# Attention loads as transfers over 128 partitions, with heads paired by parity, in a banded attention and feed-forward kernel

## The chip, the cores and the metric

The kernel runs on one core of one Trainium2 chip. The metric is the device time of one execution in microseconds (us), the median over several runs; lower is better. The profile shows one execution of its own. Engines are named as the profile names them: PE (matrix products), DVE, ACT and POOL (vector, scalar and general work), SP (here it only issues DMA transfers). The 16 DMA engines of the core move data between the chip's main memory (HBM) and the on-chip memory of 128 partitions.

## The reference: what is computed

Two stages. The first is attention with a band: 8 batches of 576 positions, 8 heads of width 64, and each position sees itself and the 63 positions before it. The second is a feed-forward layer over the 4608 resulting tokens, with a leaky slope per hidden unit.

```python
scores = scale * np.matmul(q, k.transpose(0, 1, 3, 2))
mask = (rel >= 0) & (rel < 64)
scores = np.where(mask, scores, -1000000000.0)
attn = np.exp(scores - np.max(scores, axis=-1, keepdims=True))
attn = attn / (np.sum(attn, axis=-1, keepdims=True) + 1e-09)
x = (attn @ v)                      # to 4608 x 512
h = x @ w_in                        # 4608 x 2048
g = np.maximum(h, 0.0) + alpha * np.minimum(h, 0.0)
out = g @ w_out                     # 4608 x 512
```

All of it is in float32. The feed-forward weights are split in the kernel into a high and a low part, and each product is the sum of three.

## The kernel before, in words

**Tiles.** The 4608 tokens are 36 tiles of 128, in nine groups of four (NBLK). Attention of a tile `t` (function `attend`) reads its queries `q`, the keys `k` of its two blocks of 64 positions and the block before them, and the values `v` of the same blocks. PE makes the scores `s` (32 small products), DVE masks them and takes the maximum, ACT exponentiates, DVE and POOL normalise, PE (for tiles 0 to 7) or DVE (later tiles) transposes the weights into `pt`, PE multiplies with the values into `av`, ACT and DVE split the result into `xh` and `xl`.

**Cells.** The feed-forward of a group is 16 cells (function `cell`), one for each 128 hidden units `f`. A cell makes `h` on PE (from `xh`, `xl`, `win_h`, `win_l`), `g`, `gh` and `gl` on ACT, DVE and POOL, and adds twelve products to `o` on PE (`wout_h`, `wout_l`). For the first four `f` group 0 runs two cells of two tiles each. PE is in order: cells of a group, with the attention steps of later tiles between them.

**Weights.** 32 weight tiles of 512 KB (function `weights`; tile c is `w_in` for even c, `w_out` for odd c, and belongs to f = c / 2) are fetched into `raw`, of which there are three buffers, and converted by ACT, DVE and POOL: `two`, `low`, `val`, then `win_h` and `win_l`, or `wout_h` and `wout_l`. A cell needs both tiles of its f. This happens once, during group 0.

**Loads.** In the host's arrays a head pair `e` holds two heads; `qT` and `kT` have 64 rows (the head's width) for each pair, `vN` has 64 rows (the positions of a block) for each pair and each block. In the chip's memory the pairs 0 and 1 of q and k lie in partitions 0 to 63 and the pairs 2 and 3 in 64 to 127, and the values of a tile's first block lie in the lower half, those of the block after it in the upper. Each half is a DMA of its own: four for q and k of a tile and two for its values. The first four tiles are loaded two at a time (`span`). All are issued by SP, except the keys of the first two tiles, which ACT issues. A value buffer is reused by the next tile, so in the steady stage values can load only after the previous tile's `av`.

**What sets the order.** Every piece of work is a `Step` with engines, times, predecessors and buffers. `Plan.order` places the steps greedily by their modelled times, and the resulting order is the order of the program on each engine, SP among them. A load's `moved` is its modelled transfer time; the model has one common transfer lane, and at most eight transfers in flight (FLIGHT). The program waits through eight DMA semaphores, taken in turn, so an issue can wait for the transfer eight places earlier to land. A buffer named `z...` is used by the first loads and then inherited by the last weights (`LATE`).

Of the kernel before, what the change touches and what calls it, by code (L numbers as in the profile page):

```python
# [44 lines left out]
class Plan:  # L45
# [107 lines left out]
def banded_attention_then_prelu_ffn(  # L153
# [85 lines left out]
    def weights(c):  # L239
# [80 lines left out]
    def attend(t, by_pe, want, loads_behind=(), behind=(), last=None):  # L320

        d = st[t]
        early = t < 2
        wb, pb = Buffer("w", 2 if by_pe else 1), Buffer("pt", 1)

        span = 2 if t < NBLK else 1
        own = t % span
        t0 = t - own
        if own == 0:
            if span == 2:  # L330
                j = t // 2
                qb = kb = Buffer(f"z{2 + j}", 2, f"late z{2 + j}")
                vb = Buffer(f"z{j}", 2, f"late z{j}")
            else:
                qb, kb, vb = Buffer("q", 1), Buffer("k", 1), Buffer("v", 1)
            NW = 2 * span + 1
            loads, lv = [], []

            def rooms():
                if span == 2:  # L340
                    both = room(qb, [P, 2, span * 2 * P + NW * 2 * W], F32, f"qk_{t}")
                    d["q"], d["k"] = both[:, :, :span * 2 * P], both[:, :, span * 2 * P:]
                else:
                    d["q"] = room(qb, [P, 2, span * 2 * P], F32, f"q_{t}")
                    d["k"] = room(kb, [P, 2, NW * 2 * W], F32, f"k_{t}")

            for x in range(2):
                r = slice(x * D, (x + 1) * D)

                def load_q(e, x=x, r=r):  # L350
                    if x == 0:
                        rooms()
                    nc.sync.dma_start(d["q"][r], qT[2 * x:2 * x + 2, :, t:t + span].rearrange("e d t h q -> d e (t h q)"))

                def load_k(e, x=x, r=r):
# [3 lines left out]
                loads.append(step({SP: (0.62, 0.62)}, load_q, (), [*loads_behind, *loads[-1:]],  # L359
                                  take=([qb] if span == 2 else [qb, kb]) if x == 0 else [], moved=0.88 if span == 2 else 0.6))  # L360
                loads.append(step({ACT if t == 0 else SP: (0.62, 0.62)}, load_k, (), [*loads_behind, *loads[-1:]],
                                  moved=1.02 if span == 2 else 0.73))
            for u in range(2):
                def load_v(_, u=u):
                    if u == 0:
                        d["v"] = room(vb, [P, NP, 2 * span, P], F32, f"v_{t}")
                    nc.sync.dma_start(d["v"][u * W:(u + 1) * W].rearrange("w c b d -> w c (b d)"),
                                      vN[:, :, 2 * t + u:2 * t + u + 2 * span].rearrange("c w b d -> w c (b d)"))
                lv.append(step({SP: (0.62, 0.62)}, load_v, (), [*loads_behind, *lv[:1]], take=[vb] if u == 0 else [],
                               moved=1.76 if span == 2 else 1.18))  # L370
            d["from"] = loads, lv, qb, kb, vb
        loads, lv, qb, kb, vb = st[t0]["from"]

        banks = [Buffer("o" if early else "bank", NP) for _ in range(2)]

        def score(_):
            d["w"] = room(wb, [P, NH, KW], F32, f"w_{t}")
            for x in ("nm", "sm", "rc"):
                d[x] = sb.tile([P, NH], F32, tag=f"{x}{t % 2}", name=f"{x}_{t}")
            d["s"] = [bank(banks[x], [P, 2, 2, KW], F32, f"s_{t}_{x}") for x in range(2)]  # L380
            q = st[t0]["q"].rearrange("p y (t h q) -> p y t h q", h=2, q=P)
            k = st[t0]["k"].rearrange("p y (b h w) -> p y b h w", h=2, w=W)
            for u in range(2):
                for y in range(2):
                    for h in range(2):
                        for x in range(2):
                            r = slice(x * D, (x + 1) * D)
                            nc.tensor.matmul(d["s"][x][h * W:(h + 1) * W, u, y], q[r, y, own, h, u * W:(u + 1) * W],  # L388
                                             k[r, y, 2 * own + u:2 * own + u + 2, h, :], start=True, stop=True)

        cold = 1.0 + 0.9 * (t < 2)
        sc = step({PE: (1.05 * cold, 1.15 * cold)}, score, loads, behind, take=[*banks, wb],
                  give=[qb] if qb is kb else [qb, kb])
        sc.tiled = True
        if last:
            follow(sc, last)
# [1 line left out]
        for u in range(2):  # L398
            some = []
            for e in range(NP):  # L400
                g = u * NP + e

                def mask(_, u=u, e=e, g=g):
                    m = masks[:, 1 if (t * P + u * W) % seq == 0 else 0, :]
                    nc.vector.tensor_tensor_reduce(  # L405
                        out=d["w"][:, g, :], in0=d["s"][e // 2][:, u, e % 2], in1=m, op0=ALU.add, op1=ALU.min,
                        scale=-SCALE, scalar=3.0e38, accum_out=d["nm"][:, g:g + 1])
# [6 lines left out]
                m = step({DVE: (0.21, 0.37)}, mask, [sc], give=[banks[e // 2]])  # L414
                some.append(step({ACT: (0.385, 0.58)}, soft, [m]))
            sums.append(some)

# [56 lines left out]
        def value(_):  # L474
            d["av"] = av = bank(ab, [P, NP, P], F32, f"av_{t}")
            for e in range(NP):
                for u in range(2):
                    for h in range(2):
                        r = slice(h * D, (h + 1) * D)
                        nc.tensor.matmul(av[r, e, u * W:(u + 1) * W], st[t0]["v"][:, e, 2 * own + u, r],  # L480
                                         d["pt"][:, u * NP + e, h * W:(h + 1) * W], start=True, stop=True)

        def x_high(_):
# [1 line left out]

        def x_low(_):
            nc.vector.tensor_tensor(out=xl[:, :, xs], in0=d["av"], in1=xh[:, :, xs].bitcast(F32), op=ALU.subtract)  # L487

        va = step({PE: (1.08 * cold, 1.2 * cold)}, value, lv + ready, take=[ab], give=[vb, pb])
        va.tiled = True  # L490
# [207 lines left out]
```

## Time and profile before

| what | value |
|---|---|
| median of 3 runs | 920.09 us (919.77 to 922.85) |
| the profiled execution, its own time | 917.98 us |
| its span, first to last instruction | 916.2 us |
| PE busy | 892.2 us, 97% of the span |
| DVE, ACT, POOL busy | 445.6, 382.7, 313.6 us |
| packets moved | 54121, 69.42 MB |
| queue of SP's transfers | 53728 packets, 67.78 MB, 26.5% of 16 engines' span |

An engine's busy time is the sum of its instructions; it is an average over stages with different limits. PE's row in the strip of 40 slices reads `4799999999999999999999999999999999999998`: it is less than 90% busy in the first two slices and the last. The strip of the DMA engines reads `9787645021312123212311131213121221001001`, busy in the first 160 us and light after. "Share" of the DMA engines is the mean busy share of the 16. A wait is written as "who waited <- for whom: us in all, times, longest". In rows of the trace the first two numbers are the start and the length in us.

### The profile page before, as it was taken

The numbers are of one execution on the slowest core, as the hardware profiler recorded it, in microseconds if no ns is written. First come the engines' busy times: TensorE is split into PE (matmuls) and PEld (weight loads), VectorE is DVE, ScalarE is ACT, GpSimd is POOL, SyncE is SP. The second block draws the span as 40 slices with busy tenths as digits, with TensorE's granted clock in tenths as the row PEclk, the third lists the DMA queues.
The fourth block names the chain that finished last, engine by engine and source line by source line (L and its number), as shares of the span: only waits on it lengthen the run. The fifth ranks groups of instructions, "written<-read, shape, count | busy, mean of one in ns | idle before, by whom it ended". The sixth has DMA issues, their size and how long they took to land.

```text
span 916.2 us, 15392 instructions
## 1 busy us (share of the span) xinstructions
PE 892.2 (97%) x5873; PEld 727.5 (79%) x5873; DVE 445.6 (49%) x1315; ACT 382.7 (42%) x1020; POOL 313.6 (34%) x243
## 2 busy tenths in 40 slices
PE   4799999999999999999999999999999999999998
PEld 3687778888888888888888888888888888888886
DVE  3988984644544444444444444445444544422111
ACT  3887874333433343333433333334333433322222
POOL 3677783223322332233222333233323332322221
PEclk9999999999999999999999999999999999999999
DMA  9787645021312123212311131213121221001001
GB/s 224 180 219 205 198 144 151 24 53 52 99 53 52 52 56 96 52 52 52 98 34 42 38 92 52 53 53 99 53 52 53 70 80 53 1 1 47 1 1 46
DMA packets 54121, 69.42 MB, mean 76 GB/s; under 512 B 4368, under 2 KB 45344, under 8 KB 54048
## 3 DMA queue, kind: packets, MB, share of 16 engines
q1 hardware_dynamic: 53728, 67.78, 26.5%
q8 instruction: 46, 0.75, 0.3%
q10 hardware_dynamic: 320, 0.66, 0.3%
q14 instruction: 27, 0.22, 0.1%
HBM read 58.99 MB, written 9.44 MB: 75 GB/s over the span
## 4 chain that ended last, share of the span: by engine, by line
PE 90%; DMA 3%; ACT 3%; DVE 2%; issue 1%; POOL 1%; POOLq 0%; SPq 0%; ACTq 0%; DVEq 0%
PE h L519 42%; PE o L552 41%; PE av L480 4%; PE s L388 3%; DMA raw<-w_in 1%; DMA qk<-kT 1%; DMA raw<-w_out 1%; PE t L444 1%; ACT w L411 1%; ACT low L273 0%; ACT win_h L296 0%; DVE val L277 0%; POOL val L281 0%; DVE two L260 0%; DVE win_l L300 0%
## 5 line engine op out<-in xcount | busy, mean ns | idle before, releaser
L537 POOL TENSOR_TENSOR gl<-g,gh 128x512 fp32r<-128x512 f32 (+1 forms) x135 | 173.3, 1284 | 421.7 <-ACT gh L533 421.6
L528 DVE SCALAR_TENSOR_TENSOR g<-h,s_sb,g 128x512 f32<-128x512 f32 (+1 forms) x148 | 108.9, 736 | 292.2 <-ACT g L525 291.9
L525 ACT ACTIVATE g<-h,sa_sb 128x512 f32<-128x512 f32 (+1 forms) x148 | 100.3, 678 | 334.5 <-PE h L519 332.4
L552 PE MATMUL o<-wout_h,gh 128*128 128x512 f32 x576 | 226.6, 393 | 0.0
L552 PE MATMUL o<-wout_l,gh 128*128 128x512 f32 x576 | 226.3, 393 | 0.0
L519 PE MATMUL h<-xh,win_h 128*128 128x512 f32 (+1 forms) x592 | 160.2, 392 | 3.7 <-DVE xl L487 1.8
L465 DVE STREAM_TRANSPOSE pt<-w 32x256 f32<-32x256 f32 x336 | 146.6, 436 | 31.0 <-POOL w L427 26.1
L552 PE MATMUL o<-wout_h,gl 128*128 128x512 f32 x576 | 160.6, 392 | 0.4 <-POOL gl L537 0.4
L519 PE MATMUL h<-xl,win_h 128*128 128x512 f32 (+1 forms) x592 | 155.3, 384 | 0.0
L519 PE MATMUL h<-xh,win_l 128*128 128x512 f32 (+1 forms) x592 | 154.8, 383 | 0.0
L411 ACT ACTIVATE w<-w,nm 128x128 f32<-128x128 f32 x288 | 112.1, 392 | 62.7 <-DVE nm L405 62.7
L533 ACT CAST gh<-g 128x512 fp32r<-128x512 f32 (+1 forms) x148 | 90.0, 608 | 107.4 <-DVE g L528 107.3
L519 PEld LDWEIGHTS h<-xh,win_h 128*128 128x128 f32 x592 | 106.6, 188 | 27.9 <-DVE xl L487 1.9
L552 PEld LDWEIGHTS o<-wout_h,gl 128*128 128x128 f32 x576 | 108.2, 188 | 25.0 <-POOL gl L537 0.8
L519 PEld LDWEIGHTS h<-xl,win_h 128*128 128x128 f32 x592 | 109.5, 188 | 22.9
L519 PEld LDWEIGHTS h<-xh,win_l 128*128 128x128 f32 x592 | 109.5, 188 | 22.1
L552 PEld LDWEIGHTS o<-wout_h,gh 128*128 128x128 f32 x576 | 108.2, 188 | 23.6 <-ACT g L525 0.3
L552 PEld LDWEIGHTS o<-wout_l,gh 128*128 128x128 f32 x576 | 108.2, 188 | 23.2
L427 POOL TENSOR_TENSOR w<-w,rc 128x1024 f32<-128x1024 f32 (+1 forms) x44 | 70.6, 1607 | 150.5 <-DVE rc L423 149.2
L405 DVE CUSTOM_DVE_ANT_0 w<-s,masks 128x128 f32<-128x128 f32 x288 | 63.9, 286 | 68.0 <-PE s L388 68.0
L411 ACT ACTIVATION_READ_ACCUMULATOR w<-w,nm 128x1 f32 x288 | 54.5, 189 | 0.0
L281 POOL TENSOR_TENSOR val<-val,low 128x512 int32<-128x512 int32 x32 | 42.6, 1339 | 12.5 <-DVE val L277 8.4
(48 smaller groups left out, 460.5 us busy)
## 6 DMA issues: line engine op xcount, KB each, us to landing
v<-vN SPq DMA_DIRECT2D x64, 256.0 KB, 4.2
k<-kT SPq DMA_DIRECT2D x64, 192.0 KB, 3.5
out<-os SPq DMA_DIRECT2D x36, 256.0 KB, 2.2
raw<-w_in SPq DMA_DIRECT2D x16, 512.0 KB, 4.7
raw<-w_out SPq DMA_DIRECT2D x16, 512.0 KB, 4.4
q<-qT SPq DMA_DIRECT2D x64, 128.0 KB, 3.1
v<-vN SPq DMA_DIRECT2D x4, 512.0 KB, 11.6
qk<-qT SPq DMA_DIRECT2D x4, 256.0 KB, 9.1
```

Source lines behind the costliest of these rows:

```text
L281: nc.gpsimd.tensor_tensor(out=d["val"], in0=d["val"], in1=d["tail"], op=ALU.add)
L405: nc.vector.tensor_tensor_reduce(out=d["w"][:, g, :], in0=d["s"][e // 2][:, u, e % 2], in1=m, op0=ALU.add, op1=ALU.min, scale=-SCALE, scal ...
L411: nc.scalar.activation(w, w, AF.Exp, scale=-1.0, bias=d["nm"][:, g:g + 1], accum_out=d["sm"][:, g:g + 1])
L427: nc.gpsimd.tensor_tensor(out=w, in0=w, in1=d["rc"][:, g].unsqueeze(2).broadcast_to(list(w.shape)), op=ALU.mult)
L465: nc.vector.transpose(d["pt"][ks, :, r], d["w"][r, :, ks])
L480: nc.tensor.matmul(av[r, e, u * W:(u + 1) * W], st[t0]["v"][:, e, 2 * own + u, r], d["pt"][:, u * NP + e, h * W:(h + 1) * W], start=True, ...
L519: nc.tensor.matmul(ph[:, :nt], weight(wt, f)[:, c * P:(c + 1) * P], xt[:, c, xs], start=(k == 0), stop=(k == 3 * NP - 1))
L525: nc.scalar.activation(d["g"], d["h"][:, :nt], AF.Copy, scale=sa_sb[:, f:f + 1])
L528: nc.vector.scalar_tensor_tensor(out=d["g"], in0=d["h"][:, :nt], scalar=s_sb[:, f:f + 1], in1=d["g"], op0=ALU.mult, op1=ALU.max)
L533: nc.scalar.copy(d["gh"], d["g"])
L537: (nc.gpsimd if e == POOL else nc.vector).tensor_tensor(out=d["gl"], in0=d["g"], in1=d["gh"].bitcast(F32), op=ALU.subtract)
L552: nc.tensor.matmul(po[t][0], gt[:, i * P:(i + 1) * P], weight(wt, f), start=(f == 0 and k == 0), stop=(f == NF - 1 and k == 2))
```

## The change

Loads of queries, keys and values are written anew.

- **Queries and keys.** Pairs go to the halves by parity: pair `2y + x` lies in half `x` at place `y`. The rows of both halves then follow one another at one stride in HBM, and one DMA over 128 partitions brings the q of a tile and one its k.
- **Values.** One DMA for each head pair. Its destination is 128 partitions; its source is written by hand as `[[P, 2], [row stride, 64], [1, 256]]`: two halves whose starts differ by one block, 64 rows, and 256 numbers in a row. The second half reads one block on, so the two overlap.
- **One queue.** All of these are issued by SP. Tiles are loaded one at a time, the first four too. Rooms for the first tiles are given by a table (`ROOMS`), and the late parts of the weights are eight pieces of two hidden blocks instead of four pieces of four or five.
- **Scores.** Pair `e` is found in bank `e % 2` at place `e // 2`, where it was the other way round.
- **The planner's figures.** Initial times of the engines, `moved` of the weight tiles and of the loads.

```diff
-        free = {e: 0.0 for e in (PE, DVE, ACT, POOL, SP)}
+        free = {PE: 0.0, DVE: 0.0, ACT: 0.8, POOL: 3.6, SP: 0.8}
...
-LATE = (("wout_h", 12, "z0"), ("wout_l", 12, "z1"), ("win_h", 11, "z2"), ("win_l", 11, "z3"))
+LATE = (("wout_h", 12, "z0"), ("wout_h", 14, "z1"), ("wout_l", 12, "z2"), ("wout_l", 14, "z3"),
+        ("win_h", 12, "z4"), ("win_h", 14, "z5"), ("win_l", 12, "z6"), ("win_l", 14, "z7"))
+ROOMS = {0: ("q", "k", "z0"), 1: ("q", "k", "z1"), 2: ("z4", "z5", "z2"), 3: ("z6", "z7", "z3")}
...
-        s0 = step({SP: (0.4, 0.4)}, fetch, take=[raw], moved=1.3 if odd else 2.4)
+        s0 = step({SP: (0.4, 0.4)}, fetch, take=[raw], moved=1.27 if odd else 1.47)
...
-                    nc.sync.dma_start(d["q"][r], qT[2 * x:2 * x + 2, :, t:t + span].rearrange("e d t h q -> d e (t h q)"))
...
-                    (nc.scalar if e == ACT else nc.sync).dma_start(
-                        d["k"][r], kT[2 * x:2 * x + 2, :, 2 * t:2 * t + NW].rearrange("e d b h w -> d e (b h w)"))
...
-                    nc.sync.dma_start(d["v"][u * W:(u + 1) * W].rearrange("w c b d -> w c (b d)"),
-                                      vN[:, :, 2 * t + u:2 * t + u + 2 * span].rearrange("c w b d -> w c (b d)"))
...
+            (nc.scalar if e == ACT else nc.sync).dma_start(
+                d["q"], qT[:, :, t].rearrange("(y x) d h q -> (x d) y (h q)", x=2))
...
+            nc.sync.dma_start(d["k"], kT[:, :, 2 * t:2 * t + 3].rearrange("(y x) d b h w -> (x d) y (b h w)", x=2))
+
+        loads = [step({SP: (0.62, 0.62)}, load_q, (), loads_behind, take=[qb], moved=0.75),
+                 step({SP: (0.62, 0.62)}, load_k, (), loads_behind, take=[kb], moved=1.05)]
+        lv = []
+        for e in range(NP):
+            def load_v(_, e=e):
+                if e == 0:
+                    d["v"] = room(vb, [P, NP, 2, P], F32, f"v_{t}")
+                src = vN[e, :, 2 * t:2 * t + 2].rearrange("w b d -> w (b d)")
+                src = bass.AP(src.tensor, src.offset, [[P, 2], *map(list, src.ap)])
+                nc.sync.dma_start(d["v"][:, e].rearrange("p b d -> p (b d)"), src)
+            lv.append(step({SP: (0.62, 0.62)}, load_v, (), [*loads_behind, *lv[:1]], take=[vb] if e == 0 else [],
+                           moved=0.38))
...
-                        out=d["w"][:, g, :], in0=d["s"][e // 2][:, u, e % 2], in1=m, op0=ALU.add, op1=ALU.min,
+                        out=d["w"][:, g, :], in0=d["s"][e % 2][:, u, e // 2], in1=m, op0=ALU.add, op1=ALU.min,
```

The order that the planner makes changes with it. Of three places the rows are shown; the first number of a name is the tile, or for `raw` the weight tile c.

SP before, from the start of the program up to the weight tile raw_3 (the keys of tiles 0 and 1 are on ACT's queue):

```order
L353 DMA qk_0_96<-qT 64x2x512 x2
L367 DMA v_0_101<-vN 64x4x512 x2
L249 DMA raw_0_104<-w_in 128x4x256
L353 DMA qk_2_108<-qT 64x2x512
L356 DMA qk_2_108<-kT 64x2x640
L353 DMA qk_2_108<-qT 64x2x512
L356 DMA qk_2_108<-kT 64x2x640
L249 DMA raw_2_117<-w_in 128x4x256
L249 DMA raw_1_141<-w_out 128x1024
L367 DMA v_2_173<-vN 64x4x512 x2
L249 DMA raw_4_248<-w_in 128x4x256
L249 DMA raw_3_366<-w_out 128x1024
```

SP with the change, up to the same weight tile; four rows stand ahead of these, k and q of tile 0 and of tile 1:

```order
L348 DMA v_0_104<-vN 128x1x256 x4
L251 DMA raw_0_137<-w_in 128x4x256
L337 DMA k_2_139<-kT 128x2x384
L332 DMA q_2_141<-qT 128x2x256
L348 DMA v_1_165<-vN 128x1x256 x4
L251 DMA raw_1_186<-w_out 128x1024
L337 DMA k_3_192<-kT 128x2x384
L251 DMA raw_2_199<-w_in 128x4x256
L332 DMA q_3_212<-qT 128x2x256
L348 DMA v_2_219<-vN 128x1x256 x4
L348 DMA v_3_265<-vN 128x1x256 x2
L251 DMA raw_3_302<-w_out 128x1024
```

Ahead of raw_3 stood four value DMAs of 512 KB and now stand fourteen of 128 KB; raw_4 has moved behind it.

DVE before, around the split `xl` of tile 1 (`w_3` are the masks of tile 3, `pt` copies of transposed weights, `two` the first conversion of a weight tile):

```order
L405 ISA w_3_306,nm_3_307<-s_3_1_311,masks_64 128x128
L405 ISA nm_3_307 128x1
L451 COPY pt_0_92<-t_2_0_372 128x512
L487 TENSOR_TENSOR xl_91<-av_1_334,xh_90 128x4x128
L451 COPY pt_0_92<-t_2_1_385 128x512
L422 TENSOR_SCALAR rc_3_309<-sm_3_308 128x4
L423 RECIPROCAL rc_3_309<-rc_3_309 128x4
L260 TENSOR_SCALAR two_4_414<-raw_4_248 128x512
L260 TENSOR_SCALAR two_3_435<-raw_3_366 128x512
```

DVE with the change, first where the conversion of raw_3 begins (eight masks of tile 3 follow it, with `val` of raw_2 between), then around the same `xl`:

```order
L399 TENSOR_SCALAR rc_2_244<-sm_2_243 128x4
L400 RECIPROCAL rc_2_244<-rc_2_244 128x4
L262 TENSOR_SCALAR two_3_366<-raw_3_302 128x512
L382 ISA w_3_336,nm_3_337<-s_3_0_340,masks_64 128x128
L382 ISA nm_3_337 128x1
```

```order
L399 TENSOR_SCALAR rc_3_339<-sm_3_338 128x4
L400 RECIPROCAL rc_3_339<-rc_3_339 128x4
L267 TENSOR_SCALAR two_3_366<-two_3_366,flip_sb_84 128x512
L464 TENSOR_TENSOR xl_91<-av_1_368,xh_90 128x4x128
L262 TENSOR_SCALAR two_4_424<-raw_4_362 128x512
```

The first conversion of raw_3 stood five rows behind `xl` of tile 1 and now stands ahead of it and ahead of the masks of tile 3.

PE, whose order up to the first cell is the same in both; with the change it reads there (`h_0_0` is the first cell's):

```order
L457 MATMUL av_1_368<-pt_0_92,v_1_165 64x64 x16
L421 MATMUL t_2_0_404<-ident_79,w_2_241 128x128 x4
L421 MATMUL t_2_1_417<-ident_79,w_2_241 128x128 x4
L497 MATMUL h_0_0_426<-xh_90,win_h_86 128x256 x4
L497 MATMUL h_0_0_426<-xl_91,win_h_86 128x256 x4
L497 MATMUL h_0_0_426<-xh_90,win_l_87 128x256 x4
```

Nothing has moved here: the first cell stands behind `av` of tile 1 and the transposes of tile 2, and reads the `xl` of tiles 0 and 1.

Further on, SP issues the values of tile 4 between raw_10 and raw_9, those of tile 5 around raw_16, those of tile 6 around raw_23, and those of tile 7 behind raw_31, the last weight tile.

More of the change, by code (lines that the diff above doesn't have):

```diff
@@ L324, in attend @@
         wb, pb = Buffer("w", 2 if by_pe else 1), Buffer("pt", 1)
[L326 to L352, printed above, removed]
-                    nc.sync.dma_start(d["q"][r], qT[2 * x:2 * x + 2, :, t:t + span].rearrange("e d t h q -> d e (t h q)"))
-                def load_k(e, x=x, r=r):
-                    (nc.scalar if e == ACT else nc.sync).dma_start(
-                        d["k"][r], kT[2 * x:2 * x + 2, :, 2 * t:2 * t + NW].rearrange("e d b h w -> d e (b h w)"))
[L359 to L367, printed above, removed]
-                                      vN[:, :, 2 * t + u:2 * t + u + 2 * span].rearrange("c w b d -> w c (b d)"))
-                lv.append(step({SP: (0.62, 0.62)}, load_v, (), [*loads_behind, *lv[:1]], take=[vb] if u == 0 else [],
-                               moved=1.76 if span == 2 else 1.18))
-            d["from"] = loads, lv, qb, kb, vb
@@ L372, in attend, with load_q, load_k @@
-        loads, lv, qb, kb, vb = st[t0]["from"]
+        qb, kb, vb = (Buffer(z, 1, "late " + z if z[0] == "z" else None) for z in ROOMS.get(t, ("q", "k", "v")))
+        def load_q(e):
+            d["q"] = room(qb, [P, 2, 2 * P], F32, f"q_{t}")
+            (nc.scalar if e == ACT else nc.sync).dma_start(
+                d["q"], qT[:, :, t].rearrange("(y x) d h q -> (x d) y (h q)", x=2))
+        def load_k(_):
+            d["k"] = room(kb, [P, 2, 6 * W], F32, f"k_{t}")
+            nc.sync.dma_start(d["k"], kT[:, :, 2 * t:2 * t + 3].rearrange("(y x) d b h w -> (x d) y (b h w)", x=2))
@@ L380, in score @@
             d["s"] = [bank(banks[x], [P, 2, 2, KW], F32, f"s_{t}_{x}") for x in range(2)]
-            q = st[t0]["q"].rearrange("p y (t h q) -> p y t h q", h=2, q=P)
-            k = st[t0]["k"].rearrange("p y (b h w) -> p y b h w", h=2, w=W)
+            q = d["q"].rearrange("p y (h q) -> p y h q", h=2)
+            k = d["k"].rearrange("p y (b h w) -> p y b h w", b=3, h=2)
             for u in range(2):
@@ L387, in score @@
                             r = slice(x * D, (x + 1) * D)
-                            nc.tensor.matmul(d["s"][x][h * W:(h + 1) * W, u, y], q[r, y, own, h, u * W:(u + 1) * W],
-                                             k[r, y, 2 * own + u:2 * own + u + 2, h, :], start=True, stop=True)
+                            nc.tensor.matmul(d["s"][x][h * W:(h + 1) * W, u, y], q[r, y, h, u * W:(u + 1) * W],
+                                             k[r, y, u:u + 2, h, :], start=True, stop=True)
         cold = 1.0 + 0.9 * (t < 2)
-        sc = step({PE: (1.05 * cold, 1.15 * cold)}, score, loads, behind, take=[*banks, wb],
-                  give=[qb] if qb is kb else [qb, kb])
+        sc = step({PE: (1.05 * cold, 1.15 * cold)}, score, loads, behind, take=[*banks, wb], give=[qb, kb])
         sc.tiled = True
@@ L412, in soft @@
                                          accum_out=d["sm"][:, g:g + 1])
-                m = step({DVE: (0.21, 0.37)}, mask, [sc], give=[banks[e // 2]])
+                m = step({DVE: (0.21, 0.37)}, mask, [sc], give=[banks[e % 2]])
                 some.append(step({ACT: (0.385, 0.58)}, soft, [m]))
@@ L479, in value @@
                         r = slice(h * D, (h + 1) * D)
-                        nc.tensor.matmul(av[r, e, u * W:(u + 1) * W], st[t0]["v"][:, e, 2 * own + u, r],
+                        nc.tensor.matmul(av[r, e, u * W:(u + 1) * W], d["v"][:, e, u, r],
                                          d["pt"][:, u * NP + e, h * W:(h + 1) * W], start=True, stop=True)
```

1 line of the change is left out of this document (added).

## The prediction

> **What bounds the kernel now.** I read the busy time of each engine by stretches of the span first, because a share of the whole span hides stages.
>
> ```profile
> core 0: us, PE busy (x) PEld busy (x) DVE busy (x) ACT busy (x) POOL busy (x), PEclk, DMA share, GB/s
> 0.00:31.00 31.00, 17.17 (x218) 13.65 (x219) 16.17 (x92) 16.69 (x65) 11.98 (x21) 1.00 0.94 218
> 31.00:61.00 30.00, 25.69 (x238) 22.18 (x237) 26.27 (x61) 24.55 (x67) 23.25 (x20) 1.00 0.78 214
> 61.00:140.00 79.00, 77.22 (x514) 61.54 (x512) 70.14 (x150) 61.15 (x139) 60.54 (x48) 1.00 0.59 172
> 160.00:900.00 740.00, 740.00 (x4719) 604.83 (x4719) 321.98 (x983) 267.73 (x720) 208.68 (x151) 1.00 0.18 52
> 900.00:917.00 17.00, 12.07 (x52) 9.15 (x50) 2.89 (x4) 3.80 (x6) 2.58 (x2) 0.96 0.16 62
> ```
>
> From 160 to 900 us PE never rests, at a granted clock of 1.00. It idles 13.8 us in the first 31 us, 4.3 in the next 30, 1.8 up to 140. So a change of loads counts in two ways: it moves the start-up, whose every lost microsecond is carried to the end by an engine that never rests again, or it makes a load late in the steady stage. The chain of waits shows what the start-up waits for:
>
> ```profile
> 1.96 7.57 DMA qk<-kT
> ...
> 9.55 12.64 DMA raw<-w_in
> ...
> 22.30 0.63 ACT two L258
> ```
>
> Two transfers fill 20 of the first 22 us: the first queries and keys, then the weight tile raw_2, which lands at 22.2. The DMA engines are the bound there (share 0.94), and everything behind that is a chain of conversions on DVE, ACT and POOL.
>
> **The change part by part: what a load costs.** Three stretches give the price of a byte on one DMA engine:
>
> ```profile
> 18.00:20.00 2.00, 1.63 (x19) 1.11 (x19) 1.58 (x5) 0.96 (x4) 1.08 (x2) 1.00 1.05 204
> 58.00:60.00 2.00, 2.00 (x10) 1.65 (x9) 1.98 (x4) 2.00 (x6) 2.00 (x2) 1.00 0.99 356
> 200.00:300.00 100.00, 100.00 (x654) 81.69 (x654) 46.14 (x143) 37.56 (x104) 29.14 (x21) 1.00 0.21 59
> ```
>
> Share times 16 engines over GB/s: 44.5 ns per 1000 bytes in 58 to 60, where 128-row weight tiles travel; 82 ns in 18 to 20, where loads of 64 rows travel; 57 over the steady loads. I take 44.5, the nearest to loads of 128 rows, and keep 57 and 82 as other ends. So queries and keys over all 128 rows should gain: the same bytes at almost half the price.
>
> The values are another matter. Their new source is 2 x 64 x 256: the 2 steps by one block and overlaps, so no single stride describes rows 0 to 127, and the 2 stays a level of its own, outermost. The destination counts 128. Every load of before counts the same on both sides, 64 or 128. If a transfer is dealt to the engines along its outermost level, by shares that fit both sides, 64 and 128 give sixteen shares, and 2 against 128 gives **two**. I forecast this. For it speaks that placement already follows rows and not bytes (the two prices above, at the same full share of 16 engines); no transfer of before has unequal counts, so nothing there settles it.
>
> The Trainium skill (DMA: Bandwidth & Descriptors, section "Why a DMA increments its semaphore by 16 and not by 1") states such a rule: the number of engines is the largest up to 16 that divides the slowest dimension above 1 of both sides. By it a values load runs on two engines, which gives the sum below; with sixteen it would be the first rival's. No run here shows it yet.
>
> A values DMA is 128 packets of 1 KB; on two engines each takes 64, 65,536 bytes at 44.5 ns per 1000: 2.92 us. A tile's four stand one behind the other in the same two engines' lists: 11.7 us, against 1.46 for the same 512 KB over sixteen. All other loads take a place in these lists too, behind them.
>
> **Part A, up to the first cell of the feed-forward.** The SP rows of the change (shown above) put fourteen values DMAs ahead of raw_3. Work of the two engines up to raw_3, by bytes per engine: four k 4.4 us (24,576 bytes each), four q 2.9 (16,384), fourteen v 40.9, four weight tiles 5.8 (32,768). Sum 54.0; the first packets move at about 2.0, so raw_3 lands at **56**. The lists are not empty in between: SP waits there only for the landing of the transfer eight places before, and eight of these hold ten microseconds of work or more.
>
> ```profile
> 20.20 0.37 SPq L249 DMA_DIRECT2D raw<-w_in  x1
> 29.39 0.35 SPq L249 DMA_DIRECT2D raw<-w_out  x1
> ```
>
> ```profile
> raw<-w_out SPq DMA_DIRECT2D x16, 512.0 KB, 4.4
> ```
>
> Before, raw_3 was issued at 29.4 and landed 4.4 later. It also stood behind xl of tile 1 on DVE; now its first conversion stands ahead of it, with the masks of tile 3 between. So xl of tile 1, and the first h on PE behind it, wait for raw_3:
>
> ```profile
> L277 DVE SCALAR_TENSOR_TENSOR val<-raw,two 128x512 int32<-128x512 int32 x10 | 6.6, 674 | 0.1
> ...
> L265 DVE TENSOR_SCALAR two<-two,flip_sb 128x512 int32<-128x512 int32 x4 | 3.0, 748 | 0.1
> ...
> L487 DVE TENSOR_TENSOR xl<-av,xh 128x512 fp32r<-128x512 f32 x4 | 2.7, 686 | 0.4 <-ACT xh L484 0.3
> ...
> L260 DVE TENSOR_SCALAR two<-raw 128x512 f32<-128x512 f32 x3 | 2.1, 686 | 0.2 <-DMA raw<-w_out 0.2
> ```
>
> ```profile
> 28.42 0.29 DVE L405 CUSTOM_DVE_ANT_0 w<-s,masks 128x128 f32<-128x128 f32 x1
> 28.63 0.08 DVE L405 DVE_READ_ACCUMULATOR2_ANT nm<- 128x1 f32 x1
> 28.63 0.29 DVE L405 CUSTOM_DVE_ANT_0 w<-s,masks 128x128 f32<-128x128 f32 x1
> ...
> 30.87 0.36 PE L519 MATMUL h<-xh,win_h 128*128 128x256 f32 x1
> ```
>
> One `two` 0.69, eight masks at 0.21 from start to start 1.7, val 0.67, `two` 0.75, xl 0.69: 4.5 us, and two small instructions on rc between. The first h starts at 56 + 5 = 61 instead of 30.9. PE's order up to it is the same in both programs (same rows, same places), so PE loses **30 us** here. With 57 ns the list takes 69 and the loss is 45.
>
> **Part B, the remaining weights.** v_4, v_5 and v_6 stand on SP among the last 22 weight tiles; each holds the two lists 11.7 us. What can cover that is landed weights. A cell of four tiles takes PE 5.5 us and two weight tiles:
>
> ```profile
> 78.99 2.75 PE o L552 x12
> 81.74 2.76 PE h L519 x12
> ```
>
> ```profile
> SPq L249 <- DVE val L277: 63.3, 21, 7.6
> ```
>
> SP fetches a weight tile as soon as one of three raw buffers is free, so at most three tiles are in stock: 1.5 cells, 8.3 us. Each values tile therefore costs between 3.4 and 11.7 us. PE comes from a starved stage and uses each pair as it lands; I take half a cell, 2.7, as the cover: 9.0 each, **27 us**; ends 10 and 35. v_7 stands behind the last weight tile, and group 0's last cells hide it: nothing, at most 4.
>
> **What costs nothing.** SP issues 72 q and k DMAs instead of 134 and 144 v ones instead of 68; it has room, since it waits 63.3 us for raw buffers alone in the row above. The heads change places between the score banks: the same 32 matmuls and eight masks. The late halves of the weights come in eight pieces of two instead of four, the same instructions on the same engines; the planner shifts some `gl` from DVE to POOL and weight remainders the other way, under PE's cover from 61 us on, and if that cover is gone it is a 1.3 us operation here and there. The lower price of q and k brings the first scores forward by about 5 us, which PE then spends waiting for values and weights: no gain.
>
> **The steady stage.** A tile's values may load once the previous tile's values are used:
>
> ```profile
> 308.89 0.60 SPq L367 DMA_DIRECT2D v<-vN  x1
> ```
>
> ```profile
> v<-vN SPq DMA_DIRECT2D x64, 256.0 KB, 4.2
> ```
>
> ```profile
> 305.77 1.15 PE L480 MATMUL av<-pt,v 128*64 128x64 f32 x32
> ...
> 330.09 1.09 PE L480 MATMUL av<-pt,v 128*64 128x64 f32 x30
> ```
>
> Issued at 308.9 and landed 4.2 later, they wait 17 us for their use at 330.1. On two engines they land 11.7 - 1.5 = 10.2 later; 6.8 us are left. Covered, up to 18.5 us for 256 packets, 72 ns a packet.
>
> **Sum.** The profiled execution took 917.98 us (span 916.2). With 30 + 27 it is 975; the median of the runs shown is 2.1 above the profiled one, so I give **977**.
>
> **Rivals.** (1) *Sixteen engines after all: faster.* Then fourteen v DMAs ahead of raw_3 cost 14 x 8 packets, 5.1 us instead of 40.9: raw_2 lands at about 16 instead of 22.2, raw_3 at 20, the first h at 25 instead of 30.9. The gain is 6 to 8 us of PE's 13.8 us of early idle: 913. The turning point is the number of engines: with eight it is about even, since raw_3 comes at 25 and the first h at 30; with four, at 36 and 41, some 10 slower, 930. For it speaks that 64-row loads are really dear now; against it the 2 on the outside. The Trainium skill (same page, "Rules for kernel authors") says of two transfers to disjoint partition halves that they share the engines anyway and to use one over 128 partitions. The rows agree that halves are dear; by that alone it would be this case.
> (2) *The two engines are slower than 72 ns a packet.* At the 82 ns per 1000 bytes of 18 to 20 us (84 a packet), part A grows by 896 x 38 ns = 34, part B by 30, and each of 27 steady tiles waits 3.1 us: 1124. For it: two engines alone fetch rows far apart. Against: the dear price belongs to many engines writing half the rows.
> (3) *Stock covers the values tiles in part B*: 10 instead of 27, 960; inside my range.
>
> **How the numbers follow.** Two engines within my bounds 0.80; two engines and slow 0.03; sixteen 0.12; eight 0.02, four 0.03. The chances 0.80 and 0.12 are my judgement of the access pattern. Low end: with a packet 10% cheaper A is 26, with full cover B is 10, and a PE that has just been starved may not repeat the 6.1 us that it idles between 31 and 140 now: 920 + 30 = 950, and 945 for the rounding of all three. High end: 57 ns gives A 45 and B 3 x (14.9 - 2.7) = 37: 1002; B without any cover 45: 1010; with v_7's 4, 1015. That leaves out the other cases, 2 in 10, so the range stops there. Faster by over 0.5% (what a measurement of this kernel can tell from no change): 0.12; within: 0.02; slower: 0.86.
>
> **What would show it.** Right: a values load takes over 10 us from issue to landing, the DMA share falls to a quarter or less in the first 55 us while PE idles, raw_3 lands near 56, the first h starts near 61, three gaps of about 9 us follow on PE before 170, and from then on PE is full. A landing of 3 to 4 us for values proves the two engines wrong, and the time would be near 913. PE idle in every steady tile, in front of av, would mean case 2.

## The result, and the profile after

The changed kernel takes 977.47 us (median of 4 runs, 976.44 to 977.78); the kernel before, beside it on the same chip, 920.29 (919.77 to 922.85, 4 runs). The ratio is 1.0613, 95% interval [1.0592, 1.0635]: slower, by 57 us. The profiled execution took 976.44 us, with a span of 974.6.

First the busy time of each engine by stretches of the span, in the changed kernel (PEclk is the granted clock, the share of full speed at which PE is let run):

```profile
core 0: us, PE busy (x) PEld busy (x) DVE busy (x) ACT busy (x) POOL busy (x), PEclk, DMA share, GB/s
0.00:31.00 31.00, 9.56 (x141) 7.72 (x141) 10.05 (x65) 8.21 (x34) 8.04 (x17) 0.75 0.44 137
31.00:61.00 30.00, 6.67 (x79) 5.37 (x80) 8.72 (x31) 11.67 (x43) 6.85 (x6) 0.56 0.36 119
61.00:65.00 4.00, 4.00 (x48) 3.71 (x48) 2.86 (x7) 2.41 (x6) 1.08 (x1) 0.69 0.06 24
65.00:140.00 75.00, 57.58 (x381) 47.13 (x380) 48.65 (x105) 46.10 (x110) 45.79 (x38) 0.86 0.51 162
140.00:200.00 60.00, 52.23 (x360) 41.28 (x359) 39.46 (x89) 37.28 (x86) 38.94 (x30) 0.94 0.40 127
200.00:900.00 700.00, 700.00 (x4565) 571.30 (x4564) 321.66 (x1000) 261.39 (x722) 200.28 (x143) 1.00 0.18 58
```

From 200 to 900 us PE is busy in all of it, as before, and in the tail behind that it idles 4.2 us (4.1 before). All that was lost lies ahead of 200 us. PE now idles 44.8 us in the first 61 us (before: 18.1), 17.4 from 65 to 140 (1.8 up to there before) and 7.8 from 140 to 200 (none before). And the DMA engines, which were the bound of the start with a share of 0.94, are now busy at 0.44 and 0.36 of sixteen: PE waits for loads, and the engines that could bring them are idle.

The first h of the feed-forward, and what it waited for, on DVE and on PE (start, duration, and in brackets the idle time ahead with what ended it):

```profile
55.27 0.69 DVE L262 TENSOR_SCALAR two<-raw 128x512 f32<-128x512 f32 x1 [14.33 <-DMA raw<-w_out]
...
58.97 0.73 DVE L267 TENSOR_SCALAR two<-two,flip_sb 128x512 int32<-128x512 int32 x1
59.60 0.68 DVE L464 TENSOR_TENSOR xl<-av,xh 128x512 fp32r<-128x512 f32 x1
```

```profile
60.34 1.22 PE L497 MATMUL h<-xh,win_h 128*128 128x256 f32 x4 [1.08 <-DVE xl L464]
```

DVE idles 14.33 us until raw_3 lands at 55.3, works off the masks of tile 3 and the conversions, and 5.1 us later the first h starts, at 60.34. Before it started at 30.87: 29.5 us are lost here. The rest of the span took 28.9 us longer than before (914.3 from there to the end, against 885.3). The timeline of PE behind that point shows four waits of more than 1 us:

```profile
95.51 1.12 PE L421 MATMUL t<-ident,w 128*128 128x128 f32 x4 [7.67 <-DVE two L262]
...
126.15 1.98 PE L366 MATMUL s<-k,q 64*64 64x128 f32 x32 [8.41 <-issue]
...
156.43 1.10 PE L366 MATMUL s<-k,q 64*64 64x128 f32 x32 [1.99 <-DVE g L506]
162.74 2.04 PE L497 MATMUL h<-xh,win_h 128*128 128x512 f32 x4 [5.21 <-DVE val L279]
```

Their sum is 23.3 us. What stands ahead of each is seen on SP (its queue of issues, start and time of the issues of one kind together):

```profile
75.97 6.19 SPq L348 DMA_DIRECT2D v<-vN  x4
82.27 2.44 SPq L251 DMA_DIRECT2D raw<-w_out  x1
...
104.18 7.32 SPq L348 DMA_DIRECT2D v<-vN  x3
...
144.24 6.36 SPq L348 DMA_DIRECT2D v<-vN  x3
150.77 2.48 SPq L251 DMA_DIRECT2D raw<-w_in  x1
```

Each time a tile's values (v_4, v_5, v_6) go out just ahead of weight tiles, and PE is short of weights 12 to 14 us after the start of these rows. The names in the brackets often point elsewhere, and a reader must follow them one step on: `two` and `val` are DVE's conversions of a weight tile, and the score at 126 us waits for a PSUM bank (where PE's results go) that such a conversion still holds. The wait of 1.99 us is put down to `g`, a step of the cell before; it is counted here with the 5.21 behind it, though a wait of 1.12 us for `g` stands at the same step in e1_wide (below) too, so that at most a part of it comes from late weights.

These rows also show something that the program's order alone does not: an issue of 128 KB of values takes SP 1.5 us (6.19 for four) and a weight tile behind them 2.4, against 0.35 to 0.37 in the rows shown of before. The same four DMAs over sixteen engines (e1_wide, below) take SP less than half a microsecond each:

```profile
41.13 1.88 SPq L347 DMA_DIRECT2D v<-vN  x4
```

How many engines a load uses can be counted. Every load leaves one small packet for each engine that it used, as the counts below and in the experiments show. The page of the changed kernel:

```profile
DMA packets 54345, 69.67 MB, mean 71 GB/s; under 512 B 2544, under 2 KB 47616, under 8 KB 54272
```

Before, 4368 packets were under 512 B, and it issued 273 DMAs: 273 x 16. Now there are 144 values DMAs and 141 others, and 141 x 16 + 144 x 2 is 2544, to the packet. The Trainium skill's rule (DMA: Bandwidth & Descriptors, section "Why a DMA increments its semaphore by 16 and not by 1"), the largest number up to 16 that divides the slowest dimension of both sides, gives these two, and the trace agrees.

The steady stage shows the speed of the two engines by themselves, in stretches of 2 us of one tile:

```profile
316.00:318.00 2.00, 2.00 (x11) 1.62 (x10) 1.02 (x5) 2.00 (x10) 0.00 (x0) 1.00 0.92 292
318.00:320.00 2.00, 2.00 (x10) 1.67 (x9) 0.96 (x3) 1.31 (x5) 0.80 (x1) 1.00 0.17 57
320.00:322.00 2.00, 2.00 (x10) 1.65 (x9) 1.01 (x3) 0.62 (x1) 2.00 (x2) 1.00 0.14 48
...
326.00:328.00 2.00, 2.00 (x10) 1.65 (x9) 1.85 (x5) 0.28 (x1) 1.30 (x1) 1.00 0.16 56
328.00:330.00 2.00, 2.00 (x10) 1.68 (x9) 0.00 (x0) 0.38 (x1) 0.00 (x0) 1.00 0.07 26
```

Queries and keys go first over all engines (292 GB/s); then the values move alone, at 48 GB/s and a share of 0.14, a little over 2/16. That is 24 GB/s for one engine, 41 to 42 ns per 1000 bytes, and 524,288 bytes take 10.9 us. SP issued them from 315.7 on, and they end at about 329, over 10 us from issue to landing; the product that needs them starts at 338.7. The steady stage is covered.

### The profile page after: what moved, and what is told of

Its sections match the earlier page's. It is cut to its first block, busy times and chain, and to the rows that moved or that the text cites. A ratio compares the mean times of both kernels' runs of the same rounds, so it can differ in the third digit from the quotient of the medians.

```text
span 974.6 us, 15353 instructions
## 1 busy us (share of the span) xinstructions
PE 900.4 (92%) x5873; PEld 733.6 (75%) x5873; DVE 442.0 (45%) x1308; ACT 384.6 (39%) x1024; POOL 317.7 (33%) x246
## 2 busy tenths in 40 slices
DMA packets 54345, 69.67 MB, mean 71 GB/s; under 512 B 2544, under 2 KB 47616, under 8 KB 54272
## 4 chain that ended last, share of the span: by engine, by line
PE 82%; DMA 5%; SPq 5%; issue 2%; ACT 2%; DVE 2%; POOL 1%; POOLq 0%; ACTq 0%; DVEq 0%
PE h L497 38%; PE o L530 37%; SPq L348 4%; PE av L457 3%; DMA raw<-w_in 3%; PE s L366 3%; DMA raw<-w_out 2%; SPq L251 1%; POOL val L283 0%; ACT two L260 0%; PE t L421 0%; DVE val L279 0%; SPq L332 0%; POOL gl L515 0%; SPq L337 0%
## 5 line engine op out<-in xcount | busy, mean ns | idle before, releaser
L515 POOL TENSOR_TENSOR gl<-g,gh 128x512 fp32r<-128x512 f32 (+1 forms) x144 | 185.3, 1287 | 439.0 <-ACT gh L511 438.9
L497 PE MATMUL h<-xh,win_h 128*128 128x512 f32 (+1 forms) x592 | 162.2, 396 | 6.6 <-DVE val L279 5.5
L530 PEld LDWEIGHTS o<-wout_l,gh 128*128 128x128 f32 x576 | 109.5, 190 | 23.3
L421 PE MATMUL t<-ident,w 128*128 128x128 f32 x64 | 12.4, 326 | 46.5 <-DVE nm L382 13.8
L366 PE MATMUL s<-k,q 64*64 64x128 f32 x1152 | 43.8, 295 | 12.1 <-issue 8.4
```

The lines of the kernel that those rows point to most:

```text
L497: nc.tensor.matmul(ph[:, :nt], weight(wt, f)[:, c * P:(c + 1) * P], xt[:, c, xs], start=(k == 0), stop=(k == 3 * NP - 1))
L515: (nc.gpsimd if e == POOL else nc.vector).tensor_tensor(out=d["gl"], in0=d["g"], in1=d["gh"].bitcast(F32), op=ALU.subtract)
L530: nc.tensor.matmul(po[t][0], gt[:, i * P:(i + 1) * P], weight(wt, f), start=(f == 0 and k == 0), stop=(f == NF - 1 and k == 2))
```

## The experiments

All are made from the changed kernel; where nothing else is said only the values loads differ. "Wide" stands for values with the one-stride source of e1_wide.

**Sixteen engines (e1_wide).** The array of values holds the second half's rows too, already shifted by a block, so that the source is 128 rows at one stride. That makes the array twice as large in HBM. There are the same 144 DMAs of the same bytes in the same order.

```diff
-                src = vN[e, :, 2 * t:2 * t + 2].rearrange("w b d -> w (b d)")
-                src = bass.AP(src.tensor, src.offset, [[P, 2], *map(list, src.ap)])
+                src = vN[e, :, 2 * t:2 * t + 2].rearrange("p b d -> p (b d)")
...
+    vs = np.ascontiguousarray(np.concatenate([vs[:, :, :nb], vs[:, :, 1:]], axis=1))
```

> The change with one edit: the values array holds each row of the upper half a second time, so that a values load's source is 128 rows at one stride and no longer 2 x 64. Same 144 values DMAs of 128 KB, same order on every engine. Theory (each values load was on two engines): the lists get 0.36 us instead of 2.92 us a load, the first h starts near 25, 913 us (908 to 918), faster than the kernel before. Rival (the number of issues on SP, 144 instead of 68, is what costs): 970 to 980, as the change.

Measured: 915.67 us (912.62 to 917.52), ratio to the kernel before 0.9956 [0.9938, 0.9974]. Packets under 512 B: 4560, which is 285 x 16. The first h starts at 27.62. So all of the loss, and the sign with it, hangs on how this one source is described.

**Four and eight engines (e2_four, e3_eight).** The array is padded so that the source has 4 x 32 or 8 x 16 rows, with a gap between the pieces that keeps the outermost level apart.

```diff
+                src = vN[e, :, :32, 2 * t:2 * t + 2].rearrange("g r b d -> g r (b d)")
+                src = bass.AP(src.tensor, src.offset, [list(x) for x in src.ap])
```

> As e1_wide, but the array is padded so that the source is 4 x 32 rows. Theory (shares follow the outermost count that fits both sides): four engines, 1.46 us a load; raw_3 near 36, first h near 41, 930 to 938. Rival (any source that is not one stride falls to two engines): 977.

> As e2_four with 8 x 16 rows. Theory: eight engines, 0.73 us a load; raw_3 near 25, first h near 30, 915 to 922, about the time of before. Rival (one stride or two engines): 977.

Measured: 943.58 us (ratio 1.0264 [1.0244, 1.0285]) and 926.13 (1.0074 [1.0054, 1.0095]). The packets under 512 B are 2832 = 141 x 16 + 144 x 4 and 3408 = 141 x 16 + 144 x 8. So the outermost level of the source sets the number of engines in all four cases, and time follows it. Both ran past the upper end of what was expected, by 6 and 4 us. With four, raw_3 comes at 38.0 and the first h at 43.1 (the prediction's rival had 36 and 41); and, which that rival had left out, the later waits for weights are still there, smaller:

```profile
74.56 0.89 PE L421 MATMUL t<-ident,w 128*128 128x128 f32 x4 [4.34 <-DVE two L262]
101.36 1.98 PE L366 MATMUL s<-k,q 64*64 64x128 f32 x32 [6.31 <-issue]
```

**The two parts one at a time (e4_first_wide, e5_first_two, e6_late_two).** A second array, vW, holds the values as in e1_wide; the number of the tile chooses (NBLK is 4). The condition below is e4's; e5 has `t < NBLK`, e6 `t >= 2 * NBLK`.

```diff
+                if t >= NBLK:
+                    src = vN[e, :, 2 * t:2 * t + 2].rearrange("w b d -> w (b d)")
+                    src = bass.AP(src.tensor, src.offset, [[P, 2], *map(list, src.ap)])
+                else:
+                    src = vW[e, :, 2 * t:2 * t + 2].rearrange("p b d -> p (b d)")
```

> Values of tiles 0 to 3 with the one-stride source of e1_wide, all later tiles on the change's source. Theory: part A of the loss goes, part B stays: e1's time + 27, 936 to 944. Rival (the loss is made in the steady stage or by part A alone): 960 or more in the first case, 913 in the second.

> The values loads of tiles 0 to 3 read the two overlapping runs as in the change (two engines), those of tiles 4 to 35 a source of 128 rows at one stride (sixteen). Theory (each part is the work in the lists of two engines, and the parts add): part A alone is paid. The version in which all are wide ran in 915.7 us, the change in 977.5, and the version with only tiles 0 to 3 wide in 943.2, so part A here is 977.5 - 943.2 = 34 and this one ends at 945 to 951 us; its first h starts at 60 to 61 us, and no gap of over 4 us is left between 66 and 200. Rival (once the first tiles are late, the lists stay long, and tiles 4 to 7 wait as in the change): 965 to 977 us, with the gaps before 170 us. Second rival (the delay of the first tiles is hidden in later idle time of TensorE): 925 to 935 us.

> The values loads of tiles 0 to 7 have a source of 128 rows at one stride, those of tiles 8 to 35 read the two overlapping runs (two engines). Theory (from 200 us on a tile's 11.7 us in two lists lie beside 20 us of TensorE work and more): the same time as with all tiles wide, 915.7, within 3 us: 913 to 919 us, with TensorE at work 100% of 200 to 900 us. Rival (each late load costs something, through SyncE that is held in the issue or through pieces that land late): 28 tiles by 0.5 us or more, 930 us and up.

Measured: with only tiles 0 to 3 wide 943.23 us (1.0261 [1.0240, 1.0281]); with only tiles 0 to 3 on two engines 951.79 (1.0340 [1.0319, 1.0360]); with only tiles 8 to 35 on two engines 915.70 (0.9948 [0.9930, 0.9966]). Set against e1_wide, the first four tiles cost 36.1 us, all later ones 27.6, and tiles 8 to 35 nothing; 36.1 + 27.6 = 63.7, where both together cost 61.8. The parts add. e5 lies 0.8 us above its range. The timelines say the same more sharply. With the first tiles wide, the first h is at 27.68, and the four waits stand there as in the change, only earlier:

```profile
63.93 1.12 PE L425 MATMUL t<-ident,w 128*128 128x128 f32 x4 [9.05 <-DVE two L263]
93.72 1.99 PE L370 MATMUL s<-k,q 64*64 64x128 f32 x32 [8.55 <-issue]
124.19 1.10 PE L370 MATMUL s<-k,q 64*64 64x128 f32 x32 [2.02 <-DVE g L510]
130.47 2.04 PE L501 MATMUL h<-xh,win_h 128*128 128x512 f32 x4 [5.17 <-DVE val L280]
```

With only the first tiles on two engines the first h is at 61.02, and the longest wait of PE between there and 175 us is 1.48 us.

**What the halves cost (e7_halves, e8_one).** e7 loads queries and keys over 128 partitions and the values as before, by halves of 64 (the first DMA below, for e = 0 and 1); e8 is e1_wide with one DMA of 512 KB a tile (the second). In both the planner's `moved` of a values load is set to match, so the order on the engines can shift as well.

```diff
+                nc.sync.dma_start(d["v"][e * W:(e + 1) * W].rearrange("w c b d -> w c (b d)"),
+                                  vN[:, :, 2 * t + e:2 * t + e + 2].rearrange("c w b d -> w c (b d)"))
...
+                nc.sync.dma_start(d["v"].rearrange("p c b d -> p c (b d)"),
+                                  vN[:, :, 2 * t:2 * t + 2].rearrange("c p b d -> p c (b d)"))
```

> Queries and keys are loaded as in the change, one DMA each over 128 partitions; the values as in the kernel before, two DMAs a tile of 64 partitions each, over sixteen engines. Theory (only the count of engines costs time; the bytes are the same): near the version with all loads over sixteen engines, 914 to 919 us. If the small gain of that version over the kernel before (915.7 against 920.0) comes from queries and keys, this one has it: 914 to 917. If it comes from the values over 128 partitions, this one ends where the kernel before does, 919 to 921 us. Rival (many small values DMAs are what the change pays for, not the engines): it would also be at 919 to 921, since this one has no more of them than the kernel before; it is told from the others by the four-piece version over sixteen engines, which has 144 of them and ran in 915.7.

> As the version with all values loads over sixteen engines (915.7 us), but a tile's values are one DMA of 512 KB over 128 partitions instead of four of 128 KB: 36 values DMAs for 144. Theory (SyncE's issues lie beside other work, and the bytes and engines are the same): 913 to 918 us, no difference. Rival a (SyncE's time in issues delays the first loads): the first h starts 1 to 3 us earlier and the time is 911 to 914. Rival b (a matmul of av can start on its quarter of the values, and now waits for the whole): 917 to 922 us.

Measured: e7 919.98 us, ratio 0.9993 [0.9982, 1.0003]; e8 916.69, ratio 0.9959 [0.9943, 0.9975]. Queries and keys over 128 partitions alone are worth nothing in the end, though the first h comes at 27.28 (before 30.87). The 0.4% of e1_wide needs the values too, and whether they go in four pieces or one makes no difference. What the halves do to the transfers is seen in the same stretch of the start, in e1_wide and then in e7:

```profile
5.00:10.00 5.00, 3.90 (x64) 3.23 (x64) 2.48 (x23) 2.19 (x11) 0.00 (x0) 1.00 1.05 349
10.00:15.00 5.00, 3.01 (x24) 2.31 (x28) 4.47 (x23) 5.00 (x24) 3.12 (x3) 1.00 1.07 389
```

```profile
5.00:10.00 5.00, 3.94 (x64) 3.22 (x64) 1.78 (x16) 2.13 (x11) 0.00 (x0) 1.00 1.07 262
10.00:15.00 5.00, 2.24 (x13) 1.51 (x12) 4.39 (x25) 4.69 (x23) 2.89 (x3) 1.00 1.14 270
```

All sixteen engines are full in both, and move 349 to 389 GB/s with loads of 128 rows, 262 to 270 where half-row values are among them. This does not explain the end times, though: the first h comes as early in e7 as in e1_wide (27.28 and 27.62). From there to the end e7 takes 890.1 us, e1_wide 886.2 and the kernel before 885.3, so e7 loses its early start behind the first h, and in which step stays open, since its order differs too.

**Work for the idle PE (e10_busy, beside the change again, e11_after_again).** In the change PE runs at a lower granted clock behind every wait (below). Transposes of the identity were put ahead of three steps, to find out what that costs (the second of the three is shown).

```diff
+            for _ in range(28 if t == 5 else 0):
+                nc.tensor.transpose(d["s"][0][:, 0, 0], ident, ident)
```

> The change, with transposes of the identity into the PSUM bank that the step then overwrites, put ahead of three steps for which TensorE waits: 45 ahead of the transposes of tile 2 (wait of 13.8 us, ending at 58.18), 28 ahead of the scores of tile 5 (8.4 us, ending at 126.15), 14 ahead of the hidden product of pair 11 (5.2 us, ending at 162.74). Nothing is left out. Theory (a TensorE that waited runs its next 5 us at a granted clock near 0.5, and that costs time): the clock of 58 to 64, 126 to 131 and 162 to 166 us rises from 0.5 to near 1, some 2 us are saved at each, and the time is 971 to 975 us where the change takes 977.5. Rival a (the lower clock is only a mark in the records, or later waits take up what is saved): 976.5 to 978.5. Rival b (the added transposes start late, since their bank comes free late, and stand in the way): 979 us or more.

> The change again, on the same chip as the version with transposes added, so that the two can be set side by side: 976 to 979 us by every theory.

Measured: 981.49 us (980.39 to 982.77) against 978.19 (976.84 to 980.19) for the change again. As a way to gain time it failed, as rival b has it: the transposes write the bank that the step waits for, so two of the three groups ran behind the wait and not in it. The first group ran in the wait, but at its beginning, and 9 us of waiting followed it. The run does put a price on the clock, since the same work now stands once behind a wait and once behind 6 us of other work. The scores of tile 5 and the first of the products behind them, in the change again (e11) and with the transposes (e10):

```profile
126.09 1.99 PE L366 MATMUL s<-k,q 64*64 64x128 f32 x32 [8.71 <-issue]
128.00 0.79 PE L530 MATMUL o<-wout_h,gh 128*128 128x512 f32 x1
...
129.88 0.56 PE L530 MATMUL o<-wout_h,gh 128*128 128x512 f32 x1
```

```profile
127.15 6.03 PE L362 MATMUL s<-ident 128*128 128x128 f32 x28 [8.40 <-DVE val L279]
133.12 1.10 PE L368 MATMUL s<-k,q 64*64 64x128 f32 x32
134.15 0.50 PE L536 MATMUL o<-wout_h,gh 128*128 128x512 f32 x1
...
135.19 0.39 PE L536 MATMUL o<-wout_h,gh 128*128 128x512 f32 x1
```

From the start of the scores to the start of the fifth product: 126.09 to 129.88 is 3.79 us, 133.12 to 135.19 is 2.07. This wait costs PE 1.7 us more than its length. (The first row of the second fence also corrects the bracket `issue` of the first: the scores wait for `val` of DVE, which holds their bank.)

**The values on another queue (e12_act).** The values of tiles 4 to 7 are issued by ACT instead of SP, so that a weight tile on SP's queue need not stand behind them.

```diff
+                q = nc.scalar if NBLK <= t < 2 * NBLK else nc.sync
+                q.dma_start(d["v"][:, e].rearrange("p b d -> p (b d)"), src)
```

> The change, but the sixteen values DMAs of tiles 4 to 7 are issued by ScalarE's queue in place of SyncE's; they read the same two overlapping runs, so they still lie on two engines, and the weight tiles stay on SyncE's queue. Theory (part B is a weight tile whose shares stand behind a tile's values in the same two lists; a DMA engine that has two queues takes them in turn, so the weights pass): the waits that end at 95, 126 and 163 us (7.7, 8.4 and 5.2 us, with 2.0 at 156) fall to under 3 us each, and the time to 955 to 965 us; the first h stays at 60 to 61 us. Rival a (an engine serves what was issued first whatever the queue, so the weights wait all the same): 975 to 980 us. Rival b (the issues hold ScalarE as they held SyncE, 6 to 7 us a tile, and the softmax and the weights that ScalarE prepares are late in its place): 970 to 985 us, with waits of TensorE put down to ScalarE, and ScalarE's own issues of 1.5 us and more in the records.

Measured: 975.29 us (974.52 to 975.79), ratio 1.0592 [1.0571, 1.0613]. That is 2 us under the change itself, but the intervals of the two ratios overlap, so no gain is shown. The time fits rivals a and b alike; the waits and the long issues on ACT are those of rival b, with something of the theory in it. Behind the first of these values SP's weight tiles now go out in 0.34 to 0.37 us each, but ACT is held in its place, and PE waits for what ACT makes. ACT's issues, and PE's waits:

```profile
77.11 5.11 ACTq L349 DMA_DIRECT2D v<-vN  x1
82.28 3.31 ACTq L349 DMA_DIRECT2D v<-vN  x1
...
104.72 7.59 ACTq L349 DMA_DIRECT2D v<-vN  x1
```

```profile
86.09 0.79 PE L531 MATMUL o<-wout_h,gh 128*128 128x512 f32 x1 [6.14 <-ACT gh L512]
...
113.88 0.80 PE L531 MATMUL o<-wout_h,gh 128*128 128x512 f32 x1 [5.03 <-ACT gh L512]
...
150.29 2.04 PE L498 MATMUL h<-xh,win_h 128*128 128x512 f32 x4 [4.98 <-DVE val L279]
```

The waits of 7.7 and 8.4 us for weights are gone, and waits of 6.1 and 5.0 us for `gh`, a copy on ACT, stand in their place; the third, 5.0 us in front of an `h`, is unchanged. A single issue held ACT for 7.6 us. That weights on the other queue pass the values is suggested by the missing waits, but not shown by itself, since part of what SP issued moved too.

## Why the prediction was right, and where its terms were off

The time came out at 977.5, where 977 was forecast. Step by step:

- **PE bounds the kernel, so what the start loses is carried to the end.** Right. PE is full from 200 to 900 us, and e4 and e5 show the losses adding to within 2 us.
- **Two engines for a values load.** Right, by the count of packets and by the 48 GB/s; with 4, 8 and 16 at the outermost level the count follows. This step decided the sign: the same program with sixteen ran in 915.67, rival (1), which had 913. One sign that the prediction named for it did not come: a DMA share of a quarter or less in the first 55 us. It was 0.44 and then 0.36, and the prediction's own terms ask for more than a quarter: 13.1 us of q, k and weights on all engines and 40.9 us of values on two of sixteen, in 54 us, are 0.34.
- **The price, 44.5 ns per 1000 bytes.** Nearly right: 41 to 42 measured in the steady stage, so a tile's values take 10.9 us and not 11.7. The dear price of 82 ns, which rival (2) put on the two engines, did not come. (It was read in a stretch in which loads of 64 rows and the weight tile raw_2 travel together, so it is a price of the mixture.)
- **Part A, 30 us.** Right: raw_3 at 55.3 for 56, first h at 60.3 for 61, 29.5 us. The chain of 5 us behind raw_3 took 5.1, and it is the chain that was named, `two`, masks, `val`, `two`, `xl`. The way to raw_3 was not as described, though: the prediction had SP wait only for the landing of the transfer eight places before. In the trace SP is in one issue after another from 3.0 to 48.8 us, and raw_3 itself goes out only at the end of that:

```profile
30.57 15.20 SPq L348 DMA_DIRECT2D v<-vN  x6
45.91 2.92 SPq L251 DMA_DIRECT2D raw<-w_out  x1
```

- **Part B, 27 us.** Right in place and sum (28.9), and right that weight tiles come late behind a tile's values; but the sum is made of other terms. Three waits of 9.0 were forecast; the waits are 7.7, 8.4 and 2.0 + 5.2, 23.3 in all. The price is most of that: with 10.9 us for a tile's values the same working gives 3 x 8.2 = 24.6. Rival (3), full cover and 960, did not come.
- **What was left out: a PE that waits runs slower afterwards.** The prediction read a granted clock of 1.00 in the kernel before and has no term for a lower one. From the first h on, in the changed kernel and in the one before:

```profile
60.34:200.00 139.66, 114.47 (x787) 92.78 (x788) 90.97 (x199) 86.44 (x202) 85.81 (x67) 0.89 0.44 143
...
900.00:974.60 74.60, 70.37 (x307) 57.13 (x305) 10.62 (x15) 17.49 (x27) 16.76 (x13) 1.00 0.04 15
```

```profile
30.87:200.00 169.13, 163.04 (x1174) 132.72 (x1173) 128.62 (x313) 110.20 (x279) 102.04 (x79) 1.00 0.53 149
...
900.00:916.20 16.20, 12.07 (x52) 9.15 (x50) 2.89 (x4) 3.80 (x6) 2.58 (x2) 0.98 0.17 65
```

  With the 700 us between 200 and 900, in which PE is always busy, that makes 884.8 us of busy time against 875.1 for the same instructions, and 29.4 us of idle time against 10.2. So part B is 19.2 us more idle time and 9.7 us more busy time. Most of the latter is the clock: busy time times the missing share of the clock, summed over slices of 1 us from 60.34 to 200, is 8.7 us, and nothing in the kernel before. (Against e1_wide, which has the order of the change and 877.3 us of busy time, the difference is 7.6.) The idle time is 8 us below the 27 of the prediction (the cheaper packets, and the 6.1 us that PE idled there before do not come again); the slower work was not in it. The two nearly cancel, and that the whole lands within a microsecond is partly luck.
- **SP's issues cost nothing.** Right in the steady stage (e6: 28 tiles on two engines, no loss). Not right as it was argued: the number of issues was counted and their length was not. In the rows shown up to 160 us SP is held 1.5 to 2.5 us in the mean at a values DMA, and in the steady stage about 6 us for a tile's four. What this holding costs in the first 160 us, apart from the full lists themselves, no run separates.
- **Queries and keys gain 5 us that are not used.** Nearly right: the scores of the first two tiles end at 9.3 us where they ended at 13.4, 4 us earlier, and PE spends them waiting for values and weights. In e7, where the values are loaded as before, the first h is 3.6 us earlier, and the end is where it was.
- **The turning points, "about even" with eight engines and 930 with four.** Too low: 926.1 and 943.6. Their start was 2 to 5 us late, and the working had no part B at all for them, though waits of 4.3 and 6.3 us for weights remain with four.

## What to carry to other kernels

Before two loads are merged into one by a hand-written access pattern, look at the outermost level of both sides: here an extra level of 2 put the transfer on two of sixteen engines, and 128 KB then have as many bytes for each engine as a megabyte over sixteen. Here it cost nothing where a load had some 10 us of slack left, and much where the loads were the bound: the same line is harmless in 28 tiles and costs 62 us in the first eight. Where the overlap can be written out in the array, the one-stride source has the merge without the price: 0.9956 [0.9938, 0.9974] of the time before.

## What the runs showed of the hardware that was not expected

- **The granted clock falls while PE waits, and takes some microseconds to come back.** In the change, stretches of ten microseconds around its waits, and the first of these stretches in the kernel before:

```profile
90.00:100.00 10.00, 4.49 (x15) 3.82 (x16) 6.12 (x12) 7.76 (x26) 4.05 (x3) 0.54 0.50 169
120.00:130.00 10.00, 3.85 (x37) 3.17 (x38) 5.00 (x21) 5.97 (x16) 5.05 (x4) 0.58 0.45 148
160.00:170.00 10.00, 7.26 (x26) 5.85 (x27) 8.94 (x30) 7.78 (x24) 6.51 (x5) 0.71 0.37 116
```

```profile
90.00:100.00 10.00, 10.00 (x73) 8.10 (x73) 8.78 (x13) 8.66 (x16) 7.63 (x7) 1.00 0.92 267
```

  After 8.7 us of waiting the scores take 1.99 us instead of 1.10, and full speed is back some 4 us after the wait's end (the rows of e11 and e10 above). That wait is thus paid for with 10.4 us. A wait of 1.99 us had no such price: the scores behind it took 1.10 us. The Trainium skill (TensorE: Matmul & The Clock Gate, section "Part 1: The HAM clock gate") has the half rate after idleness and some 3.4 us of work until it is lifted. The trace agrees on the half rate: in slices of 1 us the granted clock of the change is 0.50 behind the waits of 7.7, 8.4 and 5.2 us. It is back at 1.00 after 3 to 6 us of work, behind two of these three waits later than the 3.4.
- **The engine that issues a DMA can be held in the issue.** Where the values lay on two engines, an issue took SP 1.5 us in the mean of four and ACT up to 7.59 us; over sixteen it took SP 0.47 us in the mean of the same four. An engine that also computes pays for that with its own work.
- **Every engine that takes part in a DMA leaves one packet under 512 B**, so the number of engines of a load can be read from the packet counts of the page: 2544, 2832, 3408 and 4560 for 2, 4, 8 and 16.
